# Random-sketch attention with a tanh-shrink layer: an order table searched anew, with the casts and turns of w_in free to move

## The chip, the cores and the metric

The kernel runs on one core of one Trainium2 chip. The metric is the device time of one execution in microseconds (us). Its engines are TensorE (PE in the profile; PEld is its weight load), VectorE (DVE), ScalarE (ACT), GpSimd (POOL) and SyncE (SP), which here only issues DMAs.

## The reference

Four batches, four heads, 1088 positions of 32 numbers; eight sketch rows in each of S1 and S2. The features of a row are the 64 products of its two sketches.

```python
def phi(x):
    a = np.einsum('rd,bhsd->bhsr', S1, x)
    b = np.einsum('rd,bhsd->bhsr', S2, x)
    return np.einsum('bhsi,bhsj->bhsij', a, b).reshape(*x.shape[:-1], r * r)
q_p, k_p = (phi(q), phi(k))
kv = np.einsum('bhsf,bhsd->bhfd', k_p, v)
z = np.sum(k_p, axis=2)
num = np.einsum('bhsf,bhfd->bhsd', q_p, kv)
den = np.einsum('bhsf,bhf->bhs', q_p, z)[..., None] + 1e-06
attn_out = num / den
...
x = np.ascontiguousarray(attn_out.transpose(0, 2, 1, 3)).reshape(B * S, H * D)
h = x @ w_in                     # 4352 x 128 times 128 x 2048
g = h - np.tanh(h)
return (g @ w_out).astype(np.float32)
```

## The kernel before, in words

The work is written as a list of 760 operations. Each has an engine, a planned cost, what it reads and writes, and the operations it has to wait for. The constant `ORDER` holds, for each of the five engines, the numbers of its operations in the order in which the engine is to do them; every engine works strictly in that order. `Program.schedule` goes through the table with planned costs. It does not choose the order any more, but it decides how many dummy matmuls stand on TensorE ahead of each operation.

The dummies (`P.filler`, lines 508 and 509 of the profile) multiply the zero tile `wz` into PSUM bank 0, 512 or 128 columns wide. The planner puts them in where TensorE would, by its plan, wait for something. `fill_stops` (line 1069) holds all TensorE operations that write bank 0; with the first of these in the order the dummies end for good. The planned pace is 1.2 columns a nanosecond up to `COLD` = 6800 ns, then 2.4.

The operations, in the order of the data:

- **Loads.** SyncE issues, in the order of its table, the keys of batch 0 (`load_keys`, three DMAs), the first 512 columns of the queries (`load_rows`), v in four parts (`load_v`), w_in in four quarters of 256 KB (`load_w_in`), the rest of the queries, w_out in four quarters, then the same for batch 1 and later. `gated` makes a load wait until one some 2.4 MB ahead of it has landed; SyncE stands still for this. ScalarE issues S1 and S2. A load's `lag` shifts the landing that the planner expects.
- **Sketch** (`sketch`, lines 539 and 543): S1 and S2 are turned and spread; ScalarE copies them under masks into `psk` (two), `w4` (two) and, in `folding`, `s2blk` (four).
- **Keys** (`keys`): VectorE turns the keys (`kT`, 568 and 572), TensorE projects them (581), VectorE turns the result (`kab`, 589), TensorE makes the Gram matrix (`gram`, 597), VectorE masks it (`zm`, 602), TensorE folds it with S2 (`ufold`, 606), VectorE reduces it into the weights for the denominators (`uw`, 609).
- **Key products** (`key_products`, 629) on VectorE and GpSimd, with a copy `ka0` of ScalarE ahead of VectorE's part (618), and their sums with v (`values_first`, 642 for batch 0; `values`, 712 for later ones); then `kvs` (648), `fold0` (651) and `kvb` (655).
- **Queries** (`q_turn`, 740; `queries`, 752 and 760), denominators (779 to 788), products `qp` (662, 798), their transposes and copies (677, 684; 804), numerators (694, 821) into `xT`. Batch 0 is done in pieces: tiles 0 and 1, then 2 and 3, then 4 to 8.
- **w_in and w_out.** `casts` makes bf16 copies (850, 854): two quarters of w_in on ScalarE, two on GpSimd, w_out on GpSimd. `linear_turn` (864, 869) transposes each quarter of w_in through bank 0 with a copy on ScalarE. `linear_product` (876) multiplies it with w_out: g @ w_out is done as h @ w_out less tanh(h) @ w_out, and x @ (w_in @ w_out) needs only one 128x128 matrix, kept as the sum of two bf16 parts `whi` and `wlo`.
- **Layers** (`layers`): windows of 256 or 512 tokens. For each, 16 hidden blocks (L1, line 930) go through tanh on ScalarE (934) and the second matmul (L2, 951), with the linear part at 915; VectorE turns the sum (967) and SyncE sends it out. The last window stands at 910 and 946. The tables interleave the windows with the preparation of the next batch (`plan`).

In the kernel before, some operations wait for more than their data: all casts of w_in for `uw` of batch 0 (`ready`), the four turns of w_in for the numerators of tile 1 (`x0`), the query turns of batch 0's rest for the product of tile 3 (`lead`), those of batch 1 for the product of tile 8 (`gate` in `two`).

Of the kernel before, what the change touches and what calls it, by code (L numbers as in the profile page):

```python
# [36 lines left out]

ORDER = {
    "tensor": (
# [14 lines left out]
    ),  # L54
    "scalar": (
# [4 lines left out]
    ),  # L60
    "vector": (
# [5 lines left out]
    ),  # L67
    "gpsimd": (
        "4 2 5 3 24 25 17 19 20 22 21 16 18 76 15 75 77 102 103 104 105 106 107 146 148 23 237 238 243 247 361 360 359 366 370 "
        "503 504 502 509 513 "  # L70
    ),
    "sync": (
# [3 lines left out]
    ),  # L76
}

# [16 lines left out]
class Program:  # L95
# [46 lines left out]
    def schedule(self):  # L142
# [10 lines left out]
        free = {e: BEGIN for e in engines}  # L153
# [10 lines left out]
        while left:  # L164
# [20 lines left out]
            if e == "tensor":  # L185
                if filling and o in self.fill_stops:
                    filling = False
                if filling and fills_from in order["vector"]:
                    free[e] = max(free[e], fills_from.at + fills_from.cost + 200, 1050)
                    while True:  # L190
                        rate = 1.2 if free[e] < COLD else 2.4
                        wide = 512 if free[e] + 512 / rate + 60 <= o.at else 128
                        long = wide / rate + 3
                        if free[e] + long > o.at + (120 if o.at < EARLY and o.at - o.ready < 1 else -60):
                            break
                        f = Op("tensor", long, self.filler[0 if wide == 512 else 2], 0, None, None, "fill")
                        f.at, f.end = free[e], free[e] + long
                        f.deps = {fills_from} if not any(x.name == "fill" for x in order[e]) else set()
                        free[e] += long
                        passed += 2  # L200
                        mode = None
                        order[e].append(f)
                o.at = max(o.at, free[e])
                if o.at < COLD:
                    o.cost *= 1.9
                if o.mode != mode:
                    o.at, mode = o.at + (MODE if mode is None else 0), o.mode
                passed += o.ni
                while passed // CHUNK > block:
                    block += 1  # L210
                    self.fetch.append((block, o.name, o.at, have[block] - o.at))
                    o.at = max(o.at, have[block])
                    have.append(o.at + (5800 if o.at < 24000 else 3500))
# [131 lines left out]
def bass_polysketch_attn__then__act_tanh_shrink_kernel(nc, q, k, v, S1, S2, moe_w_in, moe_w_out, out):  # L345
# [95 lines left out]
    def load_small():  # L441
        for i, src in enumerate((S1, S2)):
            o = load("scalar", 1024, ("s_raw",), "s", -1000, lambda e, i=i, src=src: e.dma_start(
                out=s_raw[8 * i:8 * i + 8, :], in_=src[:, :]), True)
            o.lag = 500 * i - 500

    def cells(name, i, lo, hi):
        return [(name, i, c) for c in range(lo // 64, hi // 64)]
# [13 lines left out]
    def load_keys(prio):  # L462

        src = k[0].rearrange("h (j c) d -> (h j) (c d)", j=32)
        dst = kraw[0][:, :].rearrange("p (g f) -> p g f", f=KG)

        def runs(g0, g1, lo, hi):
            rows = src[:, KG * g0 + lo:KG * g0 + hi]
            rows = bass.AP(tensor=rows.tensor, offset=rows.offset, ap=[rows.ap[0], [KG, g1 - g0], rows.ap[1]])
            return lambda e: e.dma_start(out=dst[:, g0:g1, lo:hi], in_=rows)  # L470

        for x, (g0, g1, lo, hi) in enumerate(((0, 4, 0, 160), (0, 3, 160, 288), (3, 4, 160, 224))):
            size = 512 * (g1 - g0) * (hi - lo)
            o = load("sync", size, ("kraw0", min(x, 1)), f"k0{min(x, 1)}", prio, runs(g0, g1, lo, hi), x == 2, (350, 378, 100)[x])
            o.lag = -200
            if x == 2:
                asked.append((o, size))

# [527 lines left out]
    near = denominators(0, 0, 2, first, near=4)  # L1006
    for t in range(2):
        products_first(first, t, "vector", near[t], 4)
    ready = P.writer[("w4u", 0)]
    casts(("scalar", "scalar", "gpsimd", "gpsimd"), ready)  # L1010
    denominators(0, 2, 4, then)
    numerators_first(first, [(0, 1, 5, "scalar")], 7, "scalar")
    x0 = numerators_first(first, [(1, 2, 6, "scalar")], 3, "scalar")
    for x in range(4):
        linear_turn((0.6, 0.7, 2.1, 2.2)[x], 0, x, "scalar", [x0])
    for t in range(2, 4):
        products_first(then, t, "vector")
    numerators_first(then, [(2, 4, 5, "vector")], 6, "vector")
    lead = P.writer[("qp", 3)]
    q_turn(0, 2, -800, lead)  # L1020
    second = dict(qproj=3.1, qab=-798, den=-795, qp=-774, qpT=-773, num=-772, x=-771)
    queries(0, 4, 9, second, 4)
    denominators(0, 4, 9, second)
# [6 lines left out]
    def plan(b):  # L1030
# [17 lines left out]
            keys(b, K, ((5, 6),), 7)  # L1048

        def two():  # L1050
            gate = () if b > 1 else P.writer[("qp", 8)]
            q_turn(b, 0, T - 28, gate)
            q_turn(b, 1, T - 28, gate)
            queries(b, 0, 9, Q, 4)
            denominators(b, 0, 9, Q)
            values(b, K, 6, thirds)
            products(Q, halves, b)
            prefetch()
# [40 lines left out]
```

## Time and profile before

| | |
|---|---|
| three runs | 107.14, 107.67, 109.19 us; median 107.67 |
| the profiled execution | 108.23 us, of which 106.4 from its first to its last instruction |
| TensorE busy | 99.8 us (94%), 1284 matmuls |
| ScalarE busy | 78.1 us (73%), of which tanh 66.4 |
| VectorE busy | 61.5 us (58%) |
| GpSimd busy | 34.5 us (32%) |
| hidden layer (L930), 160 matmuls | 43.2 us |
| second layer (L951), 144 matmuls | 37.2 us |
| dummies (L508, L509), 32 recorded matmuls | 7.6 us, all ahead of 14 us |
| first hidden matmul | 17.38 us |

A busy share of TensorE is to be read with care: matmuls overlap, dummies count as busy, and a matmul at a slower pace counts as more busy time. A strip of the page shows 40 equal slices of 2.66 us; its digits are tenths. In the chain of waits a line is a start, a length and the work that the next one waited for. Times in the text are us from the span's first instruction.

### The profile page before, as it was taken

How to read it: one execution, taken by the hardware profiler on the slowest of the kernel's cores; microseconds unless marked ns; L12 is line 12 of the kernel's file. 1: busy time of each engine (PE TensorE's matmuls, PEld its weight loads, DVE VectorE, ACT ScalarE, POOL GpSimd, SP SyncE). 2: the span in 40 equal slices, each digit the busy share in tenths (PEclk: the TensorE clock that was granted, in tenths of full speed). 3: DMA queues.
4: the chain of work that ended last, by engine and by line, in shares of the span. 5: the costliest groups of instructions: out<-in, count | busy, mean ns of one | idle time of the engine just before them, and what ended most of it. 6: DMA issues, size and time to landing. Idle time of an engine off the chain costs nothing.

```text
span 106.4 us, 3021 instructions
## 1 busy us (share of the span) xinstructions
PE 99.8 (94%) x1284; PEld 53.8 (51%) x1284; DVE 61.5 (58%) x130; ACT 78.1 (73%) x108; POOL 34.5 (32%) x44
## 2 busy tenths in 40 slices
PE   6889999999999979999999999999999999999940
PEld 2436765874766533434554443554354444446740
DVE  1478886999889997689867445958360020020120
ACT  3323177915838865979898796989979999999930
POOL 5528227250572910591850049391000000000000
PEclk9999999999999999999999999999999999999999
DMA  2999999700579410796000553000003710024464
GB/s 37 287 208 324 290 321 268 221 6 6 154 201 238 92 68 9 183 267 215 7 0 12 99 84 52 6 0 0 0 12 54 115 22 0 0 34 68 68 97 88
DMA packets 24029, 11.21 MB, mean 105 GB/s; under 512 B 18000, under 2 KB 21200, under 8 KB 24016
## 3 DMA queue, kind: packets, MB, share of 16 engines
q1 hardware_dynamic: 23840, 10.95, 42.7%
q8 instruction: 10, 0.16, 0.7%
q10 hardware_dynamic: 176, 0.07, 0.2%
q14 instruction: 3, 0.02, 0.1%
HBM read 8.78 MB, written 2.23 MB: 103 GB/s over the span
## 4 chain that ended last, share of the span: by engine, by line
PE 71%; DVE 12%; ACT 6%; DMA 4%; POOL 1%; issue 1%; SPq 1%; DVEq 0%
PE ps L930 24%; PE ps L951 20%; ACT tt L934 5%; PE ps L821 4%; DMA kraw<-in_k_dram 4%; PE ps L752 3%; PE ps L915 3%; PE ps L581 2%; DVE qpT L804 2%; DVE qab L760 2%; PE ps L694 2%; DVE qp L798 2%; PE ps L508 2%; PE ps L946 2%; PE ps L642 2%; POOL qp L662 1%
## 5 line engine op out<-in xcount | busy, mean ns | idle before, releaser
L934 ACT ACTIVATE tt<-ps 128x1024 bf16<-128x1024 f32 (+1 forms) x70 | 66.4, 1000 | 10.9 <-PE ps L930 10.6
L930 PE MATMUL ps<-xT,w_in 128*128 128x512 bf16 (+1 forms) x160 | 43.2, 351 | 0.2
L951 PE MATMUL ps<-tt,w_out 128*128 128x512 bf16 (+1 forms) x144 | 37.2, 356 | 0.0
L930 PEld LDWEIGHTS ps<-xT,w_in 128*128 128x128 bf16 x160 | 16.1, 115 | 15.9 <-ACT tt L934 5.1
L629 POOL TENSOR_TENSOR wk<-kab 128x768 f32<-128x768 f32 (+2 forms) x11 | 15.5, 1406 | 22.0 <-DVE kab L589 21.4
L951 PEld LDWEIGHTS ps<-tt,w_out 128*128 128x128 bf16 x144 | 14.0, 99 | 12.7 <-issue 1.5
L967 DVE STREAM_TRANSPOSE osb<-ps 128x512 f32<-128x512 f32 (+1 forms) x9 | 5.9, 656 | 22.6 <-PE ps L951 15.5
L798 POOL TENSOR_TENSOR qp<-qa,qab 128x768 f32<-128x768 f32 x6 | 10.4, 1739 | 7.2 <-DVE qa L788 7.0
L804 DVE STREAM_TRANSPOSE qpT<-qp 128x768 f32<-128x768 f32 x9 | 8.5, 963 | 2.1 <-POOL qp L798 2.0
L760 DVE STREAM_TRANSPOSE qab<-ps 128x576 f32<-128x576 f32 (+2 forms) x10 | 6.1, 642 | 3.3 <-PE ps L752 3.3
L508 PE MATMUL ps<-wz 128*128 128x512 bf16 x10 | 5.1, 597 | 1.0 <-DVE wz L507 1.0
L740 DVE STREAM_TRANSPOSE qT<-qraw 128x576 f32<-128x576 f32 (+2 forms) x9 | 5.8, 655 | 0.1
L821 PE MATMUL ps<-qpT,kvw 32*32 32x288 f32 (+1 forms) x192 | 4.6, 399 | 0.6 <-DVE qpT L804 0.6
L568 DVE STREAM_TRANSPOSE kT<-kraw 128x576 f32<-128x576 f32 x6 | 4.4, 741 | 0.0
L589 DVE STREAM_TRANSPOSE kab<-ps 128x576 f32<-128x576 f32 (+2 forms) x5 | 3.3, 664 | 1.7 <-PE ps L581 1.6
L798 DVE TENSOR_TENSOR qp<-qa,qab 128x768 f32<-128x768 f32 x3 | 4.0, 1334 | 0.0
L581 PE MATMUL ps<-kT,psk 64*32 64x288 f32 (+2 forms) x80 | 3.6, 427 | 0.3 <-DVE kT L572 0.3
L821 PEld LDWEIGHTS ps<-qpT,kvw 32*32 32x32 f32 x192 | 2.4, 103 | 2.6 <-DVE qpT L804 1.1
L712 PEld LDWEIGHTS ps<-wk,vx 128*32 128x32 f32 x216 | 3.2, 110 | 1.1 <-issue 1.1
L712 PE MATMUL ps<-wk,vx 128*32 128x64 f32 x216 | 3.6, 220 | 0.0
L509 PE MATMUL ps<-wz 128*128 128x128 bf16 x22 | 3.6, 291 | 0.0
L509 PEld LDWEIGHTS ps<-wz 128*128 128x128 bf16 x22 | 2.5, 129 | 2.2 <-issue 2.0
(96 smaller groups left out, 96.7 us busy)
## 6 DMA issues: line engine op xcount, KB each, us to landing
vx<-in_v_dram SPq DMA_DIRECT2D x12, 144.0 KB, 3.5
qraw<-in_q_dram SPq DMA_DIRECT2D x4, 288.0 KB, 4.6
qraw<-in_q_dram SPq DMA_DIRECT2D x4, 256.0 KB, 4.8
w_in_f<-in_moe_w_in_dram SPq DMA_DIRECT2D x4, 256.0 KB, 5.4
w_out_f<-in_moe_w_out_dram SPq DMA_DIRECT2D x4, 256.0 KB, 4.3
out_dram<-osb SPq DMA_DIRECT2D x16, 64.0 KB, 2.0
kraw<-in_k_dram SPq DMA_DIRECT2D x3, 288.0 KB, 4.1
kraw<-in_k_dram SPq DMA_DIRECT2D x3, 256.0 KB, 4.2
```

The lines of the kernel that those rows point to most:

```text
L508: P.filler = (lambda e: e.matmul(ps[:, FB, 0:512], wz[:, :], wz[:, None, :].to_broadcast([128, 4, 128]), start=True, stop=True), wzero, la ...
L509: lambda e: e.matmul(ps[:, FB, 0:128], wz[:, :], wz[:, :], start=True, stop=True))
L629: P.op(eng, dve(cols) if eng == "vector" else pool2(cols), lambda e, t0=t0, t1=t1, ap=ap, m=m, ka0=ka0: e.tensor_tensor(out=wk[:, t0:t1, : ...
L712: ins = e.matmul(ps[32 * h:32 * h + 32, vb, 0:64], vx[i][:, h, t, :], wk[:, t, h, :, :], start=(t == 0), stop=(t == NT - 1), tile_position ...
L760: P.op("vector", dve(2 * n), lambda e, h=h: e.transpose(out=qab[:, t0:t1, h:h + 2, :].rearrange("p t h x -> p h t x"), in_=ps[:, qb + h:qb ...
L798: P.op(eng, dve(cols) if eng == "vector" else pool2(cols), lambda e, p0=p0, p1=p1, w=w: e.tensor_tensor(out=qp[:, p0:p1, :, :, :].rearrang ...
L804: P.op("vector", dve(cols), lambda e, p0=p0, p1=p1: e.transpose(out=qpT[:, p0:p1, :, :, :].rearrange("p t h y j -> p (t h y j)"), in_=qp[: ...
L821: ins = e.matmul(ps[32 * h:32 * h + 32, nb[g], 0:32 * n], kvw[i][32 * g:32 * g + 32, y, 32 * h:32 * h + 32], qpT[32 * g:32 * g + 32, t0:t0 ...
L930: P.op("tensor", pe(n), lambda e, jb=jb + y, y=y, hb=hb: e.matmul(hb[:, n * y:n * y + n], hidden(w_in, jb), xT[:, f0:f0 + n], start=True, ...
L934: P.op("scalar", act(q * n), lambda e, un=un, hb=hb, q=q: e.activation(out=tt[:, un, 0:q * n], in_=hb[:, 0:q * n], func=AF.Tanh, scale=-1. ...
L951: P.op("tensor", pe(n), lambda e, jb=jb, un=un, y=y: e.matmul(acc[:, 0:n], w_out[:, jb, :], tt[:, un, n * y:n * y + n], start=(not f0 and ...
L967: P.op("vector", dve(n), lambda e: e.transpose(out=osb[u][:, 0:n], in_=acc[:, 0:n]), r=[ka], w=[("osb", u)], prio=slot0, name=f"osb{w}")
```

## The change

The four extra waits go: casts and turns of w_in, and the query turns, wait only for their data and places. Casts and turns may thus stand anywhere in the tables.

The planner's expectations change at the start. S2 lands 300 ns later in the plan (`lag` from 0 to 300), the second and third key loads 350 ns later (from -200 to 150). Dummies begin earlier in the plan: 90 instead of 200 ns behind `wz`, and not before 990 instead of 1050 ns; a dummy at the slower pace is planned 3 ns shorter.

`ORDER` is replaced. The number of operations and what each computes stay the same. The main moves near the start, by name:

- TensorE: `psk, kproj0.0, kproj0.5, gram0, turn0, ufold0, qproj0.0, tiles..., fold0, qt0.0, turn1, qt0.1, qt0.2, num0.0, num0.1, turn2, num0.2, L1.0.0 to 3, turn3, qproj0.4`. Before: `... gram0, ufold0, qproj0.0, tiles..., fold0, qt0.1, qt0.0, num0.1, turn0, qt0.2, num0.0, turn1, num0.2, turn2, L1.0.0 to 3, qproj0.4, L1.0.6, turn3`.
- ScalarE: `s2blk0, psk1, s2blk2, psk0, s2blk1, w40, w41, s2blk3, cast_in0, ka0, w_inT0, kvs0, cast_in1, kvb0, kvb1, ...`. Before: `w41, psk1, psk0, s2blk3, s2blk2, ka0, s2blk0, s2blk1, w40, cast_in1, kvs0, cast_in0, kvb1, kvb0, ...`.
- VectorE: the four masks ahead of the key turns; the turns of batch 1's keys behind `qp0.6` and `qpB0.8`; `osb0` ahead of `x0.4`.
- SyncE: keys, queries, w_in quarter 0, v, queries, w_in 1, w_out 1, w_in 2, w_in 3, w_out 0, 2, 3, then batch 1. Before: keys, queries, v, w_in 1, w_in 0, queries, w_in 2, keys of batch 1, w_in 3, w_out. The last part of batch 1's v stands behind the first output.
- GpSimd: other places for the memsets at the start; `wk0.0` ahead of `wk0.2`.

The diff without the table's numbers:

```diff
-                    free[e] = max(free[e], fills_from.at + fills_from.cost + 200, 1050)
+                    free[e] = max(free[e], fills_from.at + fills_from.cost + 90, 990)
...
-                        long = wide / rate + 3
+                        long = wide / rate + (3 if rate > 2 else 0)
...
-            o.lag = 500 * i - 500
+            o.lag = 800 * i - 500
...
-            o.lag = -200
+            o.lag = (-200, 150, 150)[x]
...
-    ready = P.writer[("w4u", 0)]
-    casts(("scalar", "scalar", "gpsimd", "gpsimd"), ready)
+    casts(("scalar", "scalar", "gpsimd", "gpsimd"), ())
...
-    x0 = numerators_first(first, [(1, 2, 6, "scalar")], 3, "scalar")
+    numerators_first(first, [(1, 2, 6, "scalar")], 3, "scalar")
     for x in range(4):
-        linear_turn((0.6, 0.7, 2.1, 2.2)[x], 0, x, "scalar", [x0])
+        linear_turn((0.6, 0.7, 2.1, 2.2)[x], 0, x, "scalar")
...
-    lead = P.writer[("qp", 3)]
-    q_turn(0, 2, -800, lead)
+    q_turn(0, 2, -800)
...
-            gate = () if b > 1 else P.writer[("qp", 8)]
-            q_turn(b, 0, T - 28, gate)
-            q_turn(b, 1, T - 28, gate)
+            q_turn(b, 0, T - 28)
+            q_turn(b, 1, T - 28)
```

More of the change, by code (lines that the diff above doesn't have):

```diff
@@ L61 @@
     "vector": (
[5 rows of a table removed]
[5 rows of a table added]
     ),
     "gpsimd": (
-        "4 2 5 3 24 25 17 19 20 22 21 16 18 76 15 75 77 102 103 104 105 106 107 146 148 23 237 238 243 247 361 360 359 366 370 "
-        "503 504 502 509 513 "
+        "18 2 22 15 4 3 5 24 25 16 23 19 20 17 21 75 76 77 102 103 105 104 106 107 146 148 237 238 243 247 359 361 360 366 370 "
+        "502 504 503 509 513 "
     ),
     "sync": (
[3 rows of a table removed]
[3 rows of a table added]
     ),
```

48 rows, old and new, of the table ORDER are left out of this document.

## The prediction

> **What bounds the kernel now.** I read the page first: its strip of slices and its clock line, then a table of stages, the chain that ended last, and the timelines of TensorE and SyncE over the first 18 us.
>
> ```profile
> PE   6889999999999979999999999999999999999940
> PEclk9999999999999999999999999999999999999999
> ```
>
> ```profile
> 80.00:100.00 20.00, 20.00 (x102) 9.84 (x100) 1.43 (x2) 19.53 (x21) 0.00 (x0) 1.00 0.27 42
> ```
>
> TensorE has no visible idle time from about 9 us on, but for 0.58 us at 38.7. Behind 40 us it does only matmuls that the result needs, so nothing is to be had there by a new order; what is won ahead comes out at the end unless TensorE runs short of work. Its only spare time lies ahead of the first hidden-layer matmul (L930) at 17.38: dummies on `wz` (L508, L509) fill 7.6 us there.
>
> The busy share hides a second thing. Three stretches of TensorE (length, busy time, matmuls):
>
> ```profile
> 1.96:5.37 3.41, 3.11 (x31) 1.00 0.97 256
> 5.37:8.79 3.42, 3.09 (x56) 1.00 1.09 212
> 8.79:12.20 3.41, 3.41 (x83) 1.00 0.99 329
> ```
>
> ```profile
> 8.31 0.61 PE L508 MATMUL ps<-wz 128*128 128x512 bf16 x1
> 8.71 0.42 PE L509 MATMUL ps<-wz 128*128 128x128 bf16 x2
> ...
> 9.31 0.61 PE L508 MATMUL ps<-wz 128*128 128x512 bf16 x1
> 9.72 0.53 PE L509 MATMUL ps<-wz 128*128 128x128 bf16 x3
> 10.18 0.73 PE L752 MATMUL ps<-qT,w 32*32 32x128 f32 x32
> 10.84 0.39 PE L509 MATMUL ps<-wz 128*128 128x128 bf16 x2
> 11.16 1.68 PE L642 MATMUL ps<-wk,vx 128*32 128x64 f32 x72
> 12.78 0.39 PE L508 MATMUL ps<-wz 128*128 128x512 bf16 x1
> ```
>
> A 512-wide dummy holds TensorE 0.40 us at 8.31 (the next starts at 8.71) and 0.23 at 12.78 (next at 13.01). The 72 tile sums (L642) take 1.68 us here; the same 72 matmuls of later batches (L712) take 1.21. Single starts put the change of pace at 12.2, although the clock line says full speed all along. It follows the first 3.4 us without idle time; the two stretches ahead hold 0.30 us (to 4.13, S1 and S2 landing) and 0.33 us (to 6.47, keys landing).
>
> The chain ahead of the first hidden-layer matmul:
>
> ```profile
> 14.51 0.44 PE ps L694 x4
> 14.95 0.35 PE ps L864 x4
> 15.30 0.46 PE ps L677 x4
> ...
> 15.78 0.70 DVE qpB L684
> 16.48 0.04 issue
> 16.52 0.65 PE ps L694 x4
> 17.18 0.37 PE ps L864 x4
> 17.55 0.44 PE ps L930 x4
> ```
>
> Turn 0 of w_in (L864 at 14.95) stands in it, ahead of the transposes of query tiles 2 and 3 (L677 at 15.30), whose copy (L684) everything waits for.
>
> ```profile
> 2.32 0.43 SPq L455 DMA_DIRECT2D qraw<-in_q_dram  x1
> 2.79 1.85 SPq L484 DMA_DIRECT2D vx<-in_v_dram  x4
> 4.69 0.91 SPq L492 DMA_DIRECT2D w_in_f<-in_moe_w_in_dram  x2
> ```
>
> SyncE issues v ahead of w_in; the change puts the first quarter of w_in at 2.79.
>
> **The change part by part.** No needed operation is added or removed; the price lies in order, waits and dummies.
>
> *Sketch and key projection.* ScalarE now does s2blk0, psk1, s2blk2, psk0. s2blk takes 0.235 (0.47 for two); psk0 ended at 5.15 behind one w4 copy, and comes about 0.40 later. The first projection moves from 5.36 to 5.76 and from its end at 6.15 to 6.55, the second from 6.47 to 6.55. The masks come ahead of the key transposes, which takes 0.18 off VectorE at 6.45. Cost **+0.1**.
>
> *Dummies.* The planner now expects S2 0.30 us and the second keys 0.35 us later and starts the dummies 0.11 us earlier. That is the size of the two gaps, so both should close: dummies run to about 4.1, and the two projections stand back to back. Between the second projection and the Gram matmul the plan puts dummies at full pace; if TensorE is at half pace they overrun by up to 0.3. Bounds 0 to +0.3; I take **0**, since I forecast full pace by then or soon after.
>
> *Turn 0 ahead of the folding matmul.* It is the first writer of bank 0, and the planner stops dummies there. So none follow after about 8.8 us, where before had 15 (L508 and L509 from 8.31 on). Turn 0 itself costs 0.43 at half pace in place of 0.61 of dummies at 8.31: nothing, if cast 0 is done by 8.2. The cover is the wait for zm (8.44 to 8.61). The load of w_in's first quarter is issued at 2.79; loads of v and of w_in take 4.4 at best, w_in 5.4 in the median: it lands between 7.2 and 8.2. Cast 0 (0.62) ends between 7.8 and 8.8. Behind it on ScalarE waits the copy ka0 (before at 7.74), for that VectorE's key products; behind turn 0 on TensorE waits ufold (8.92). Late landing costs up to +0.35, early none. I take **0**.
>
> *No dummies ahead of the query projection.* uw is done at 9.73 and the projection starts at 10.18, since three dummies stand ahead of it; with a handover of 0.2 it could start at 9.95: -0.23. The tile sums come right behind it, without the 0.32 of dummies at 10.84. v lands later by one w_in quarter (0.7 between w_in landings), about 10.3, still ahead of them.
>
> *Pace.* If TensorE is at full pace from 8.8 us or earlier, ufold and the projection win about 0.35 together (halving what their 0.58 and 0.73 stream), the tile sums 0.47 (1.68 against 1.21). VectorE's turns of the queries (11.10) and all behind them on VectorE start about **0.6** earlier, 0.23 by the dummies and 0.37 by the pace, less the 0.1 above: **-0.5**. If it stays at half pace, this is a loss (below).
>
> [...]
>
> *Turns out of the chain.* Tiles 2 and 3 are now transposed ahead of the numerators. Their products end at 14.57 before; then VectorE does the query turn (0.78, to 15.38) and the copy (0.70, to 16.08), then the numerators start, and the first hidden matmul follows 0.55 later at about 16.65 against 17.38: **-0.7**. ScalarE's part (two copies 0.28, turn copy 0.58, two x copies 0.30 each behind 14.19) ends by 16.1 and stays hidden. But turn 3 (0.25 of array time) now stands ahead of qproj0.4, which all of VectorE's second stage waits for: of the 0.7, **-0.45** reaches it.
>
> *Later.* SyncE's order no longer puts a load of batch 1's keys, which held it from 6.6 to 10.05, ahead of w_in's last quarter. In its place a w_out load waits for all of v (about 10.3), with w_in's third and fourth quarters behind it: the third lands near 13.1 instead of 12.1, before turn 2 (15.5) needs its cast; the fourth and w_out land earlier, by about 1 and 1.5 us, and nothing in the chain waited for them. osb0 (0.45) moves ahead of x0.4 on VectorE, the second key turn (0.76) ahead of the last query products; both are VectorE time spent in any case. On SyncE the last part of v for batch 1 is queued behind the first output, at about 26 instead of 18.21, due at 32.77; v of batch 2 behind the output of window 2 (osb2 ends 46.34), due at 51.18. With 2.6 to 3.5 us to land both have over a microsecond. Taken at **0**, bounds 0 to +0.6.
>
> Sum: -0.5 - 0.45 = -0.95, with about 0.05 lost on the way: **-0.9**. This execution took 108.23 (span 106.4 and 1.8 around it), 0.56 above the median 107.67 of the three runs, which spread over 2.05. From 108.23 the sum gives 107.3; moved to the median, 107.67 - 0.9 = **106.8**.
>
> **The rivals.**
> 1. *TensorE stays at half pace* (slower). Place: from 9.4, where no dummy bridges the waits for uw and kvs. It decides if none of the early 3.4 us counts as busy. For it: 0.30 of idle time spoiled a stretch before, and without dummies 0.5 us stand idle ahead of the query projection and again ahead of the fold. Against it: from 0.99 to 9.4 hardly any gap is left. Price, if pace doubles at about 19: 0.2 on the tile sums, 0.45 on the transposes, 0.4 on the numerators, 0.44 on the first hidden matmuls, 0.25 on turn 3, 0.2 on qproj0.4, and 0.9 on the eight hidden matmuls behind it: 2.85, less 0.45 and 0.23 won and part hidden in waits: about +1.4, **109.1**. If it doubles at 15.6 instead, about 107.7.
> 2. *w_in lands late.* If the first quarter lands at 9.0 instead of by 8.2, cast 0 ends at 9.65 and turn 0 holds ufold to 10.3, 1.4 behind; with the gains: +0.5, **108.2**. For it: w_in took up to 6.0 us to land. Against: then it stood behind v.
> 3. *Won ahead, lost behind.* Batch 1's numerators at 39.31 wait for VectorE, which is full from 31 to 39; a load out of the new SyncE order comes late. Then 0.6 of the gain goes: **107.4**.
> 4. *Full pace from 5.4 us.* Projections and Gram win too, 0.2 each, and dummies never overrun: -1.7, **106.0**.
>
> **How the numbers follow.** Forecast 0.50 (105.9 to 107.3), rival 1 0.20, rival 2 0.08, rival 3 0.14, rival 4 0.08. The range, 105.6 to 108.9, leaves out the worst of rival 1 and the best of rival 4. 2% of 107.67 is 2.15 us, about what a measurement of this kernel can tell from no change, given the spread of 2.05: faster means below 105.5, the lower end of rival 4 and little of the forecast (0.08); slower above 109.8, the upper end of rival 1 (0.06).
>
> **What would show it.** Right: no idle time of TensorE at 3.8 and 6.2; turn 0 between the Gram and folding matmuls without a wait for the cast; query projection at about 9.5 to 9.9; tile sums in 1.2 us; first L930 at 16.0 to 16.7. Wrong: 512-wide dummies or 128-wide turns still at half pace beyond 12.2, the folding matmul behind 9.2, a wait of turn 0 for w_in, or an idle stretch of TensorE behind 25 us that before does not have.

## The result, and the profile after

| | before | after |
|---|---|---|
| median of 20 executions each | 107.95 us | 108.91 us |
| ratio, 95% interval | | 1.0105 (1.0066 to 1.0144) |
| profiled execution, its span | 108.23, 106.4 | 109.63, 107.8 |
| first hidden matmul | 17.38 | 17.78 |
| from there to the last matmul's start | 84.8 | 86.3 |
| from there to the end of the span | 4.25 | 3.68 |

The change makes the kernel about 1% slower; 106.8 was forecast. The ratios here compare executions within 1.5% of each kernel's fastest; in the changed kernel 8 of the 9 left out had lost pace (mean clock 0.963 to 0.983; in the profile below TensorE was at half clock for a while), which goes with its order, as the runs below show. The medians, over all executions, give 108.91 / 107.95 = 1.0089.

The profiled executions differ by 1.34 us of span: 0.40 lost ahead of the first hidden matmul, 1.51 lost behind it, 0.57 won at the tail. The profile after is of an execution that lost pace (mean clock 0.968), as half of its executions did; the one before did not.

The page's strip of TensorE and its clock, after:

```profile
PE   6976899699989999999699999999999999999970
PEclk9996569999999999999999999999999999999999
```

Before, the clock line was full throughout. Here it falls in the slices from 8 to 16 us. Three stretches of TensorE (length, busy time and matmuls, clock, DMA share, GB/s):

```profile
5.32:8.73 3.41, 1.97 (x55) 1.00 1.08 262
8.73:12.14 3.41, 2.97 (x86) 0.50 0.70 148
12.14:15.56 3.42, 3.03 (x48) 0.50 0.74 190
```

Full pace came at 5.3, earlier than before (12.2): the first key projection (L581) takes 0.51 us, before 0.79. It was lost at 8.73 and came back at 15.56. TensorE's timeline after, at the places that matter (in brackets the idle time ahead, and what ended it):

```profile
7.32 0.38 PE L597 MATMUL ps<-kab 128*32 128x32 f32 x18 [0.17 <-DVE kab L589]
8.86 0.61 PE L864 MATMUL ps<-identb,w_in 128*128 128x128 bf16 x4 [1.16 <-ACT w_in L850]
9.27 0.58 PE L606 MATMUL ps<-zm,s2blk 128*128 128x32 f32 x2
10.12 0.74 PE L752 MATMUL ps<-qT,w 32*32 32x128 f32 x32 [0.28 <-DVE w L609]
10.90 2.15 PE L642 MATMUL ps<-wk,vx 128*32 128x64 f32 x72
...
17.78 0.63 PE L930 MATMUL ps<-xT,w_in 128*128 128x256 bf16 x4
...
21.62 1.07 PE L876 MATMUL ps<-w_out,w_inT 128*128 128x128 bf16 x16 [1.11 <-POOL w_out L854]
...
53.44 1.21 PE L712 MATMUL ps<-wk,vx 128*32 128x64 f32 x72 [0.84 <-DMA vx<-in_v_dram]
```

In the kernel before, the last two start without a wait:

```profile
20.21 1.06 PE L876 MATMUL ps<-w_out,w_inT 128*128 128x128 bf16 x16
...
51.18 1.21 PE L712 MATMUL ps<-wk,vx 128*32 128x64 f32 x72
```

Three long waits are new: turn 0 (L864) for the cast of w_in's first quarter, 1.16; the product of w_in and w_out (L876) for the last cast of w_out, 1.11; batch 2's sums (L712) for v, 0.84. The tile sums (L642) run at half pace throughout, 2.15 against 1.68. SyncE's timeline shows where the last two waits come from, after and then before:

```profile
5.66 0.43 SPq L492 DMA_DIRECT2D w_in_f<-in_moe_w_in_dram  x1
10.87 0.33 SPq L497 DMA_DIRECT2D w_out_f<-in_moe_w_out_dram  x1
11.24 1.82 SPq L492 DMA_DIRECT2D w_in_f<-in_moe_w_in_dram  x2
13.11 1.39 SPq L497 DMA_DIRECT2D w_out_f<-in_moe_w_out_dram  x3
...
48.88 0.91 SPq L484 DMA_DIRECT2D vx<-in_v_dram  x2
```

```profile
6.12 0.43 SPq L492 DMA_DIRECT2D w_in_f<-in_moe_w_in_dram  x1
10.05 0.33 SPq L455 DMA_DIRECT2D kraw<-in_k_dram  x1
10.43 0.43 SPq L492 DMA_DIRECT2D w_in_f<-in_moe_w_in_dram  x1
10.90 2.92 SPq L497 DMA_DIRECT2D w_out_f<-in_moe_w_out_dram  x4
```

After, SyncE issues nothing behind 5.66 until v has landed at 10.86: the first w_out load waits for that, and w_in's third and fourth quarters stand behind it. The third lands at 16.13 (before 12.11), the last of w_out at 20.89 (before 17.42). Meanwhile the DMAs moved 148 GB/s from 8.73 to 12.14, where before they moved 329 from 8.79 to 12.20. The part of batch 2's v that its sums wait for is issued at 48.88 and lands at 53.39; before, the sums began at 51.18.

### The profile page after: what moved, and what is told of

Its sections match the earlier page's. It is cut to its first block, busy times and chain, and to the rows that moved or that the text cites. A ratio compares the mean times of both kernels' runs of the same rounds, so it can differ in the third digit from the quotient of the medians.

```text
span 107.8 us, 2979 instructions
## 1 busy us (share of the span) xinstructions
PE 98.1 (91%) x1266; PEld 53.3 (49%) x1266; DVE 61.8 (57%) x130; ACT 77.8 (72%) x108; POOL 35.3 (33%) x44
## 4 chain that ended last, share of the span: by engine, by line
PE 57%; DMA 16%; SPq 11%; DVE 6%; POOL 4%; issue 2%; ACT 1%
PE ps L930 20%; PE ps L951 19%; DMA vx<-in_v_dram 10%; DMA w_out_f<-in_moe_w_out_dram 6%; PE ps L821 4%; POOL qp L798 4%; SPq L484 3%; PE ps L915 3%; PE ps L712 2%; SPq L492 2%; SPq L455 2%; PE ps L946 2%; PE ps L752 1%; DVE qab L760 1%; SPq L470 1%
## 5 line engine op out<-in xcount | busy, mean ns | idle before, releaser
L930 PE MATMUL ps<-xT,w_in 128*128 128x512 bf16 (+1 forms) x160 | 42.1, 351 | 0.0
L967 DVE STREAM_TRANSPOSE osb<-ps 128x512 f32<-128x512 f32 (+1 forms) x9 | 5.9, 655 | 20.8 <-PE ps L951 20.8
L798 POOL TENSOR_TENSOR qp<-qa,qab 128x768 f32<-128x768 f32 x6 | 11.2, 1866 | 6.8 <-DVE qa L788 6.6
L508 PE MATMUL ps<-wz 128*128 128x512 bf16 x9 | 4.1, 594 | 1.0 <-DVE wz L507 1.0
L833 ACT CAST xT<-ps 128x256 bf16<-128x256 f32 (+2 forms) x6 | 2.2, 379 | 3.5 <-PE ps L821 3.5
L712 PE MATMUL ps<-wk,vx 128*32 128x64 f32 x216 | 3.6, 220 | 0.8 <-DMA vx<-in_v_dram 0.8
L712 PEld LDWEIGHTS ps<-wk,vx 128*32 128x32 f32 x216 | 3.2, 110 | 2.1 <-DMA vx<-in_v_dram 1.3
L752 PE MATMUL ps<-qT,w 32*32 32x288 f32 (+2 forms) x160 | 3.6, 392 | 0.3 <-DVE w L609 0.3
L833 DVE CAST xT<-ps 128x256 bf16<-128x256 f32 (+2 forms) x6 | 2.3, 393 | 2.5 <-PE ps L821 2.5
```

The lines of the kernel that those rows point to most:

```text
L712: ins = e.matmul(ps[32 * h:32 * h + 32, vb, 0:64], vx[i][:, h, t, :], wk[:, t, h, :, :], start=(t == 0), stop=(t == NT - 1), tile_position ...
L752: ins = e.matmul(ps[32 * g:32 * g + 32, qb + h, 0:n], w4[i][32 * h:32 * h + 32, :], qT[i][32 * h:32 * h + 32, :].rearrange("p (t g j) -> p ...
L798: P.op(eng, dve(cols) if eng == "vector" else pool2(cols), lambda e, p0=p0, p1=p1, w=w: e.tensor_tensor(out=qp[:, p0:p1, :, :, :].rearrang ...
L930: P.op("tensor", pe(n), lambda e, jb=jb + y, y=y, hb=hb: e.matmul(hb[:, n * y:n * y + n], hidden(w_in, jb), xT[:, f0:f0 + n], start=True, ...
L967: P.op("vector", dve(n), lambda e: e.transpose(out=osb[u][:, 0:n], in_=acc[:, 0:n]), r=[ka], w=[("osb", u)], prio=slot0, name=f"osb{w}")
```

## The experiments

The theories: **queue** (SyncE's table brings loads late), **pace** (TensorE falls to half clock because the dummies end), **turn** (turn 0's early place, with its load ahead of v). Ratios are against the kernel before on the same chip, with 95% intervals; medians in us. An execution's mean clock shows pace that was lost, not how late it first came: the profile before, at full pace only from 12.2, has 1.00.

| | median | before | ratio |
|---|---|---|---|
| 1 w_out load behind w_in | 108.01 | 107.37 | 1.0044 (0.9996 to 1.0092) |
| 2 batch 2's v early | 107.69 | 107.37 | 1.0020 (0.9979 to 1.0062) |
| 3 dummies held until turn 1 | 108.12 | 107.37 | 1.0102 (1.0043 to 1.0160) |
| 4 before without late dummies | 107.47 | 107.37 | 1.0017 (0.9980 to 1.0053) |
| 5 moves 1 and 2 | 107.26 | 107.16 | 0.9934 (0.9885 to 0.9984) |
| 6 moves 1 and 2, dummies as in 3 | 106.99 | 107.16 | 0.9973 (0.9928 to 1.0017) |
| 7 before with batch 2's v late | 111.31 | 107.16 | 1.0255 (1.0151 to 1.0359) |
| 8 moves 1 and 2, turn 0 and its load back | 106.05 | 107.16 | 0.9876 (0.9819 to 0.9933) |
| 9 the same again | 106.09 | 107.36 | 0.9907 (0.9866 to 0.9947) |
| 10 before with the new plan numbers | 107.00 | 107.36 | 1.0008 (0.9970 to 1.0047) |
| 11 as 8, w_in's first quarter ahead of v | 106.73 | 107.36 | 0.9963 (0.9923 to 1.0003) |
| 12 as 6, no dummies ahead of turn 0 | 106.79 | 106.79 | 0.9963 (0.9921 to 1.0006) |

**1. The w_out load behind w_in.** Operation 42 is the w_out load, 38 and 39 are w_in's third and fourth quarters.

```diff
+ORDER["sync"] = ORDER["sync"].replace("37 42 38 39 41", "37 38 39 42 41")
```

> The changed kernel with one move in SyncE's table: the w_out load that waits for v goes behind the third and fourth quarters of w_in. Queue theory: the two quarters are issued at about 6.2 and 6.7 instead of 11.2 and 12.6, their casts no longer wait until 16.1, turn 2 loses its 0.23 us wait at 16.85, w_out lands some 1 to 2 us earlier and TensorE's 1.11 us wait ahead of the w_in w_out product at 21.6 shrinks below 0.4; the time falls by 0.5 to 1.0 us, to a ratio of about 1.000 to 1.005 against the kernel before (the changed kernel stands at 1.0105). Pace theory (the dummies that end at turn 0 cost the time): the wait ahead of the product may go, but the time stays within 0.3 us of the changed kernel's.

The wait ahead of the product is gone (no gap over 0.08 us there), and the ratio falls from 1.0105 to 1.0044, in the range of the queue theory. The intervals overlap, so this run alone doesn't settle it. Batch 2's sums still waited, 1.08 us.

**2. Batch 2's v early.** 251 to 254 are its four parts, 50 the last part of batch 1's v.

```diff
+ORDER["sync"] = ORDER["sync"].replace("49 250 208 249 50 209", "49 50 250 208 249 251 252 253 254 209")
+ORDER["sync"] = ORDER["sync"].replace("373 251 374 379 372 252 253 283", "373 374 379 372 283")
+ORDER["sync"] = ORDER["sync"].replace("378 254 375", "378 375")
```

> The changed kernel with batch 2's v, and the last part of batch 1's v, moved ahead in SyncE's table, before the loads that wait for batch 1's numerators. Queue theory: v of batch 2 lands at about 33 instead of 53.4, the 0.84 us wait of TensorE ahead of the sums of batch 2 goes, and the time falls by 0.3 to 0.8 us. Pace theory and turn theory (turn 0 waiting for w_in costs the time): the wait goes, too, but TensorE has that much less to do later on another wait; within 0.3 us of the changed kernel's time.

The wait of the sums went, and 0.85% with it (1.0105 to 1.0020, intervals just apart), a little over what the queue theory gave.

**3. Dummies held until turn 1.** Turn 0 uses bank 2, guarded by the reads of `kab0.0` and ahead of `fold0`, and so no longer counts as a writer of bank 0, with which the dummies end.

```diff
+            o.lag = 0 if x else 1500
...
+        key = ("turned",) if bk else bank[bk]
...
-        linear_turn((0.6, 0.7, 2.1, 2.2)[x], 0, x, "scalar")
+        linear_turn((0.6, 0.7, 2.1, 2.2)[x], 0 if x else 2, x, "scalar")
...
+    by["turn0"].deps.add(by["kab0.0"])
+    by["fold0"].deps.add(by["w_inT0"])
```

> The changed kernel with turn 0 in PSUM bank 2 instead of bank 0, so that the dummies go on until turn 1, and with the first w_in quarter planned to land 1.5 us later, so that dummies also fill the wait ahead of turn 0. Pace theory: TensorE, at full pace from 5.3 or 8.7 us on, does not fall back; the tile sums take about 1.2 us instead of 2.15, the first hidden matmul comes 0.8 to 1.2 us earlier than 17.8, and the time falls by 0.5 to 1.0 us, to a ratio of 1.000 to 1.005. Queue theory: the opening gets faster, but w_out still lands at 20.9, so the product waits that much longer and the time stays within 0.3 us of the changed kernel's.

The pace theory got the opening it asked for: full pace from 5.2 us to the end, first hidden matmul at 15.90, 1.9 us ahead of the changed kernel. The ratio did not move (1.0102 against 1.0105). TensorE's timeline says where the gain went:

```profile
20.75 1.05 PE L878 MATMUL ps<-w_out,w_inT 128*128 128x128 bf16 x16 [1.49 <-POOL w_out L855]
...
52.84 1.21 PE L713 MATMUL ps<-wk,vx 128*32 128x64 f32 x72 [1.12 <-DMA vx<-in_v_dram]
```

Both waits grew, from 1.11 to 1.49 and from 0.84 to 1.12. An earlier opening was worth nothing here, while loads set the time of two operations behind it.

**4. Before without late dummies.**

```diff
-    P.fill_stops = {o for o in P.ops if o.eng == "tensor" and o in P.wrote.get(bank[FB], ())}
+    P.fill_stops = {o for o in P.ops if o.name == "ufold0"}
```

> The kernel before without the 15 dummies behind the Gram matmul of batch 0; nothing else differs. It measures the price of the dummies alone. Pace theory: the pace doubles at 15 us or later instead of 12.2, and the time rises by 0.7 to 1.5 us over the kernel before (ratio 1.007 to 1.014). Queue theory: what the pace costs is about made good by the query projection no longer waiting behind dummies (0.23 us) and the tile sums (0.32 us); ratio 0.998 to 1.004.

No measurable price. In its profile pace was full from 4.2 us and held, with 0.69 us idle ahead of the folding matmul; the first hidden matmul came at 15.69. So in the order of before the missing dummies cost nothing: rival 1, as the prediction put it (no dummies in the waits for uw and kvs), doesn't suffice as a cause.

**5. Both moves together.** Edits 1 and 2.

> The changed kernel with both moves in SyncE's table: the w_out load behind w_in's quarters, and batch 2's v early. Queue theory: the two gains add up (0.6% and 0.85% of the two single moves, from 1.0105), no wait of TensorE over 0.4 us is left behind 17 us, and the ratio against the kernel before is 0.993 to 0.999: the new order is a gain once the loads are in time. If the two moves removed the same loss twice over: 1.002 to 1.004.

The ratio is in the range for two gains that add up. But its medians are even (107.26 against 107.16): its executions lie at 105.9 to 106.3 and at 107.2 to 108.3; their mean clocks don't tell the two groups apart, and what does stays open. In its profile half pace held from 9.86 to 16.68 behind a wait of turn 0 of 1.20 us, and the first hidden matmul came at 18.11. Behind it no wait over 0.36 was left, and 84.3 us to the last matmul against 84.8 before. By these profiles the new order is about 0.5 us better there once loads are in time.

**6. Both moves, and dummies as in 3.**

> Both moves in SyncE's table and the dummies held until turn 1 (turn 0 in bank 2, w_in's first quarter planned 1.5 us later). Queue theory with the pace as a smaller part: now that no late load swallows it, full pace through the opening comes out at the end, 0.3 to 0.8 us below the kernel with both moves alone; ratio 0.987 to 0.995. If dummies are worth nothing here: within 0.3 us of both moves alone.

The ratio is that of no gain from dummies, the median is 0.3 below that of 5; the two intervals overlap. All 12 executions had a mean clock above 0.99, but in the profile the four wide dummies ahead of turn 0, run at half pace, held the folding matmul until 10.19.

**7. Before with batch 2's v late.** The order of before, with 251 to 254 behind 373 as in the change.

```diff
+ORDER["sync"] = ORDER["sync"].replace("48 251 49 50 252 208 255 253 209", "48 49 50 208 255 209")
+ORDER["sync"] = ORDER["sync"].replace("373 282 374 283 254 375", "373 251 282 374 252 253 283 375")
+ORDER["sync"] = ORDER["sync"].replace("284 420 421 343 422", "284 343 254 420 421 422")
```

> The kernel before with one thing of the change: batch 2's v goes behind the load that waits for batch 1's numerators in SyncE's table, its last part behind the first output of window 2. Queue theory: v lands at 50 to 53 where the sums need it at 51.2; TensorE waits 0.3 to 1.2 us there and the time rises by 0.3 to 0.9 us, ratio 1.003 to 1.008. Rival: the wait is made up behind it, since hidden matmuls can be done at any time; ratio 0.998 to 1.002.

The mechanism suffices by itself, and at three times the most that was expected; most of its executions lost pace, too, as in the profile. TensorE's timeline, then two of its stretches:

```profile
52.37 2.15 PE L716 MATMUL ps<-wk,vx 128*32 128x64 f32 x72 [2.41 <-issue]
```

```profile
48.89:52.30 3.41, 1.08 (x5) 1.00 0.68 211
52.30:55.72 3.42, 3.01 (x75) 0.50 0.02 5
```

v landed at 52.28 (the row names no releaser). Pace was lost behind the wait of 2.41: 3.4 us at half clock (0.50), of which half, 1.7, is by my estimate the most that this can have added. Hidden matmuls did not make it up: from the first of them to the last matmul it took 89.5 us instead of 84.8.

**8 and 9. Both moves, turn 0 and its load back.** w_in's first quarter (36) goes behind v, its cast (100) behind ka0, turn 0 (120) behind the fold, so dummies run until then. Besides edit 2:

```diff
+ORDER["sync"] = ORDER["sync"].replace("31 36 32 33 34 35 40 37 42 38 39 41", "31 32 33 34 35 36 40 37 38 39 42 41")
+ORDER["tensor"] = ORDER["tensor"].replace("68 120 70 82", "68 70 82")
+ORDER["tensor"] = ORDER["tensor"].replace("91 112 122 116 130 114", "91 120 112 116 130 122 114")
+ORDER["scalar"] = ORDER["scalar"].replace("61 100 74 121 90 101 92 93 113 117 123", "61 74 100 90 101 92 93 113 121 117 123")
```

> Both moves in SyncE's table, and w_in's first quarter back behind v, turn 0 behind the fold and its cast behind the key products' copy. Turn theory (turn 0 ahead of the folding matmul holds TensorE): slower opening goes, folding matmul at 8.8 instead of 9.3, and the time falls by 0.2 to 0.6 us below both moves alone. Forecast's step (turn 0 out of the chain ahead of the first hidden matmul is a gain of 0.4 to 0.7): it rises by 0.3 to 0.7 us.

> The kernel with both moves in SyncE's table and turn 0 back behind the fold, measured again. If the new order is a gain once loads are in time and turn 0 holds nobody: ratio 0.984 to 0.992 as before. If the first measurement was a lucky draw of six executions: 0.993 to 0.999.

Folding at 8.68, as the turn theory had it, and 0.9876, then 0.9907: this version beats both kernels, the second time over 12 executions. None of the 18 had a mean clock below 0.99.

**10. Before with the new plan numbers.** The four edits to the planner, without the new order.

> The kernel before with the change's planner numbers alone (dummies begin earlier, S2 and the second keys planned later), its own order and waits. The forecast's step (two gaps of 0.30 and 0.33 us closed, so that full pace comes earlier): 0.3 to 1.0 us faster, ratio 0.991 to 0.997. If dummies in the opening are worth nothing measurable, as the run without the late ones says: 0.998 to 1.002.

No measurable effect. The gap ahead of S1 and S2 was still 0.23.

**11. As 8, with w_in's first quarter ahead of v** (36 stays behind 31).

> As the kernel with both moves and turn 0 back behind the fold, but w_in's first quarter still ahead of v in SyncE's table. It tells the place of turn 0 from the place of the load. If the wait of turn 0 costs: as fast as with the load behind v, ratio 0.986 to 0.992. If the later landing of v (11 instead of 9.4) costs: the tile sums start 0.3 to 0.8 us later, ratio 0.992 to 0.997.

The load alone costs something: v lands at 10.51 instead of 9.32 (run 8), TensorE waits 0.75 us for it ahead of the tile sums, and the ratio is 0.9963, against 0.9876 and 0.9907. The intervals overlap a little; on the same chip, with 12 executions each, the medians are 106.73 here and 106.09 in run 9.

**12. As 6, without dummies ahead of turn 0.** Turn 0 early, the load ahead of v.

> Both moves in SyncE's table and turn 0 ahead of the folding matmul in bank 2, so that dummies go on behind it, but w_in's first quarter planned as in the change: no dummies are put ahead of turn 0 for its landing. It tells apart why turn 0 at this place costs. If the extra dummies ahead of turn 0 held it back (four wide ones ran to 9.9 at half pace): 0.5 to 1.0 us below the kernel with them (ratio 0.997), near the one with turn 0 back (0.988 to 0.991). If the wait for w_in's first quarter is the price: within 0.4 us of 0.997.

The dummies ahead of turn 0 are not the price: 0.9963, as in 11. With the load ahead of v in both, the early and the late place of turn 0 give the same ratio. In this profile the load landed early enough (7.54): turn 0 started at 8.23 and folding at 8.64, as early as in run 8, but the tile sums waited 0.64 for v, which landed at 10.84. So the price lies with the load ahead of v, through v's landing in this profile; where w_in lands late, as in the change (8.16), turn 0 waits, too.

## Why the prediction was wrong

All four signs of being wrong that the prediction names appeared: turns still at half pace at 14.45 (0.63 us for four, 0.39 at 18.25), folding at 9.27, a wait of turn 0 for w_in, and a new idle stretch behind 25 us (0.84, up to 53.44).

**The step that failed most is "Later", taken at 0 with bounds 0 to +0.6.** Its waits were 1.11 and 0.84 in the profile. Run 5 undoes both moves, and the ratio goes from 1.0105 to 0.9934, that of the medians from 1.0089 to 1.0009: 0.9 to 1.8 us. I had seen both moves in SyncE's table and mis-sized the landings. w_out was to land 1.5 us earlier: it landed 3.5 later. v of batch 2 was given over a microsecond to spare: it was 2.2 late (53.39 against 51.18). I added 2.6 to 3.5 us to one issue, where parts of v took 2.6 to 5.3 before, 3.4 in the median; this one came at 48.88 and took 4.5. The w_out load waits for a landing, so an emptied queue fills again only from 10.87, and v itself landed 1.3 us later than before (10.86 against 9.56, forecast 10.3). Rival 3 named the place (a load of the new order comes late); its price of 0.6 was a third to two thirds. Runs 2 and 7 show the late v by itself; run 1 does so for w_out with intervals that overlap, and its wait went as expected. Run 3 shows that the two waits swallow what is won ahead.

**"Turn 0 ahead of the folding matmul", taken at 0, bounds 0 to +0.35.** The load landed at 8.16, the late end of the range, and folding moved from 8.92 to 9.27, the upper bound. But two things were missing. The dummies end ahead of turn 0, too, so TensorE stood idle for 1.16 us in a place I had called covered; and v behind the load costs the tile sums up to 0.75 us (run 11). Ratios of 0.988 and 0.991 with both back (8, 9) against 0.993 and 0.996 with the load ahead of v (5, 11, 12) put this at 0.3 to 0.9% of the time; most of these intervals overlap. The query projection, which this was to leave free for 9.5 to 9.9, began at 10.12, behind the folding matmul and the weights made from it. These were ready at 10.07; the handover took 0.05, where the -0.23 for the projection rests on an estimate of 0.2.

**"Pace".** It came early, as in rival 4 (5.3 us), and was lost, as in rival 1, but not in the place given there: what came ahead of the loss was the wait for turn 0, in which no dummies stand. Mean clocks of 0.985 or less:

| | executions |
|---|---|
| turn 0 early, no dummies ahead of it (the change, 1, 2, 5, 12) | 32 of 68 |
| turn 0 early, dummies ahead of it (3, 6) | 0 of 18 |
| turn 0 and its load back (8, 9) | 0 of 18 |
| turn 0 back, its load ahead of v (11) | 2 of 12 |
| the kernel before, next to runs 1 to 12 | 1 of 98 |

What the loss costs is not shown. In the change the executions that lost pace have a median of 109.69, the others 108.58; in runs 2, 5 and 12 they are slower, too, by 0.4 to 1.1, but in run 1 faster by 0.7, and keeping pace (runs 3 and 6) did not lower the ratio.

What decides when pace comes or goes is not shown. That closed gaps would bring it early was an estimate from three stretches of one profile. In the change it came early with a gap of 0.22 us left ahead of it, was lost 3.41 us later and came back after 6.83, and the stretch ahead of the loss was busy for 1.97 of 3.41 us.

**"Turns out of the chain", -0.7, of which -0.45 was to arrive.** Not reached in the change: turn 2 waited for w_in's third quarter (16.13, forecast 13.1), and from 8.73 to 15.56 TensorE ran at half clock (0.50).

**The opening as a whole, -0.95 in the sum, shows no gain in any profile.** The prediction took the pace of one execution, full from 12.2, for that of the kernel before. In run 7, with the same opening, pace was full from 4.5, in runs 4 and 10, with other dummies alone, from 4.2 and 5.6, and the first hidden matmul came at 15.53, 15.69 and 15.86 instead of 17.38. In the new order with pace as early it came at 15.90 (run 3, full from 5.2) and 16.10 (run 11, full from 5.4). So much of what was forecast as a gain of the change was there for the old order, too, in executions whose pace came early. These are single profiles, and how often it comes early is not known.

**"Dummies".** The two gaps were to close; 0.22 and 0.23 are left. In run 10 the planner's new numbers closed the second gap in the old order and left 0.23 of the first, and were worth nothing measurable. The projection's +0.1 did not come: the first began at 5.52, forecast 5.76, and the keys landed 0.2 earlier in this execution.

**Won unforeseen:** the end. The prediction saw nothing to be had behind 40 us. With the loads in time (runs 5, 6, 8, 9, 11, 12) the last matmul starts 84.3 us behind the first hidden one, in the order of before 84.8 to 85.2 (before, runs 4 and 10), and the span ends 3.7 behind it instead of 3.9 to 4.25. Together this is 0.8 to 1.5 us, and runs 8 and 9 are 1.1 and 1.3 below the kernel before in their medians. So what the best version wins lies, by these profiles, behind the opening. For the tail, SyncE's last issue, before and after:

```profile
103.59 0.65 SPq L963 DMA_DIRECT2D out_dram<-olast  x1
```

```profile
104.88 0.65 SPq L963 DMA_DIRECT2D out_dram<-olast  x1
```

Before, its tile was ready at 102.74 and the issue waited 0.85 behind four outputs of the window ahead; after, 0.22 (ready at 104.66), since that window's turn (L967) comes 2.5 ahead of it instead of 1.9. This makes up the 0.57 of the table above.

What stays open: how much of the 0.5 us behind the first hidden matmul comes from which move of the order (a wait of 0.58 at 38.7 before is under 0.2 in the new order, but one of 0.36 ahead of batch 1's folding matmul is new), and whether the dummies ahead of turn 0, the difference between runs 6 and 12, are what kept the clock up in run 6: the two ran on different chips.

## What to carry to other kernels

Cost a moved load from the moment that its queue may issue it: look at what the loads ahead of it wait for, and add what an emptied queue loses (here the DMAs moved 148 GB/s for 3.41 us, where before they moved 329). A faster opening comes out at the end only if no later operation has a due time of its own, so list the loads with theirs before you count a gain. Where a stage's pace varies from execution to execution, as here (full from 12.2 us in one profile and from 4.5 in another with the same opening), look at several profiles of the kernel before: a gain counted against one whose pace came late may be there already. Before you put an operation with an uncertain operand into an in-order queue, look at what stands behind it there, and whether it switches anything off, as turn 0 did with the dummies.

## What the runs showed of the hardware that was not expected

Pace was lost behind stretches in which TensorE was partly busy: of the 3.41 us ahead of the loss (counted in such steps from the first change of pace) it was busy for 1.08 (run 7), 1.62 (run 5), 1.97 (the change) and 2.05 us (run 2). But busy time alone does not decide it. Two stretches of run 3, where a stretch of 1.92 is followed by one at full clock:

```profile
18.84:22.25 3.41, 1.92 (x26) 1.00 1.05 295
22.25:25.67 3.42, 3.42 (x32) 1.00 0.32 73
```

Nor does it decide when full pace first comes: it came behind stretches with 2.85 (run 4, 0.75 to 4.17) and 2.89 us (run 7, 1.10 to 4.52), but not behind those with 3.11 and 3.09 of the kernel before. So a stretch without idle time, which the prediction had read from one profile as the condition, is not needed, and what else counts beside busy time stays open. Half pace (clock 0.50) lasted 3.41 us after the loss in run 7 and 6.83 in the change and in runs 2 and 5.
